# A delta-rule attention with two MoE layers: the first tile's x finished in PSUM, and the second MoE's second layer turned round

## The chip, the cores and the metric

The kernel runs on one core of a Trainium2 chip. The metric is the device time of one execution in microseconds (us). The kernel before was run three times: 1483.88, 1479.08 and 1480.54 us, median 1480.54. A core has TensorE (PE, matmuls; PEld is its weight load), VectorE (DVE), ScalarE (ACT), GpSimd (POOL) and SyncE (SP), which here only issues transfers (DMAs).

## The reference

Three layers follow one another, all in fp32: attention with a state that is corrected token by token, a gated MoE without experts, and an MoE of four experts that are all computed and weighted by given probabilities.

```
B, H, S, D = 4, 8, 768, 48                       # 3072 tokens, 384 = H * D
for t in range(S):                               # per batch and head, state 48 x 48
    y[:, :, t] = q[:, :, t] @ state              # reads before it writes
    v_old = kt @ state                           # kt: k of the token / (its norm + 1e-6)
    state = state + beta * outer(kt, vt - v_old)
x = y.transpose(0, 2, 1, 3).reshape(3072, 384)
h = x @ w_in                                     # 384 -> 2048
x = (h * sigmoid(1.702 * h)) @ w_out             # 2048 -> 384
p = probs / (probs.sum(-1) + 1e-9)               # 3072 x 4
out = 0
for e in range(4):
    out += p[:, e] * (relu(x @ w1[e]) @ w2[e])   # 384 -> 1024 -> 384
```

## The kernel before

**Numbers.** Every large operand is kept as two fp32r halves, hi (the rounded value) and lo (the rest), and each product of the MoE layers is three matmuls: hi x hi, hi x lo, lo x hi (`PASSES`). A "split" makes the pair: ScalarE (or VectorE) copies to hi, VectorE subtracts for lo.

**Attention.** The sequence is cut into 12 blocks u of 64 tokens. For each block the work is: normalise k; transpose it (`queue_keys`, L333); grams of k with k and of k with q (`queue_g` L511/L514, `queue_q` L444); invert a small triangular matrix for each batch and head (on GpSimd, or for blocks 0 and 1 on VectorE in two halves that PE merges, L661/L670, `queue_first_inverse`); and then the chain (`queue_chain`), which must run block after block because of the state: product of k and the state (L733), two solves (L743) with a cross product between (L753), `read` (L765: y from state and corrected values, both kept in `su`) and `write` (L770: the state's change). The 32 states of 48 x 48 (4 batches, 8 heads) lie as two times 16: heads in pairs x = 0, 1 on partitions 0 to 47 and 64 to 111. `read` gives y with d on the partitions, which is x^T, the form that the MoE's first layer takes as moving operand. Partitions 48 to 63 and 112 to 127 stay free; of four pairs of heads three fill the 48-row places (KD = 3 blocks of 128 rows), and the fourth pair's 48 rows are cut into three times 16 for the free places. For this, `y_copy` (L180 as helper) copies y to `stage` and the fourth pair to a scratch `YS`, and six DMAs a block (`put`, L848; for blocks 0 and 1 three on SP's queue and three on ACT's) move the pieces of 16.

**First MoE.** Six tiles t of 512 tokens (two blocks each, of four batches). `split_x` splits `stage` into `xs`; for each of 16 blocks f of 128 hidden units `layer1` (L884) makes `ph`, `gate` applies the gelu and splits it into `gh` (L987, L989, L990), and `layer2_1` (L972) sums `px` with the weights as the loaded operand. The second layer is one step behind the first, so that PE has work while the gate runs. Tiles 0 and 1 begin in halves of 256 columns (`HALVED`: 8 and 16 steps), so that the first half can start when one block of attention is done. The weights of this layer come as 64-bit floats that are converted on chip (L230, L277 and others).

**Order of work.** The attention of tile t + 2 is queued when tile t starts. A list scheduler written into the kernel (`Order`, `Task`) keeps a modelled clock for each engine and gives each piece a priority; `tick` in `layer1` and `layer2_1` lets pieces of attention in between MoE matmuls, and `until` runs the list up to given pieces. The resulting order on each engine is fixed when the kernel is built.

**Second MoE.** It runs expert by expert (e), tile by tile (t), in 8 steps f. The weights of all eight steps of an expert stay resident; those of the next are split during tile 5 (`queue_w2`). x of the tile is split two steps ahead (`split_now`, L1077/L1078) into one of two sets of buffers, `xsp` and `xs2`. `layer1` is the same function as in the first MoE, then a relu with split (L1112, L1113), and, a step later, `layer2_2` (L1086): for each batch b three matmuls of 384 columns with the hidden values as loaded operand, so that tokens lie on the partitions, into four of six PSUM buffers `po`. At the last step VectorE multiplies by the probability of each partition's token and adds to `oacc` (L1094), and for the last expert four DMAs write a tile. Between the two MoEs the PSUM pools change: `ps2`'s buffers can be used when the last `px` has been copied out, and VectorE does that copy after the three splits of the second MoE's first x.

Of the kernel before, what the change touches and what calls it, by code (L numbers as in the profile page):

```python
# [149 lines left out]
def delta_attention_moe_moe_kernel(  # L150
# [17 lines left out]
    E = probs.shape[1]  # L168
    F2 = we.shape[0] // E
# [52 lines left out]

    def load_w2(n):
        nc.sync.dma_start(out=raw[:, n % 2, :], in_=we[n])

    def split_w2(n):
        t = wp.tile([128, 2, 768], F32R, name="w", tag="w")
        half = raw[:, n % 2, :]
# [94 lines left out]
    V = nc.vector  # L323

# [98 lines left out]
    def queue_q(u):  # L423
# [11 lines left out]
        for g0 in range(0, NP, 8):  # L435
# [251 lines left out]
    def queue_chain(u):  # L687
# [27 lines left out]
        for hu in range(2):  # L715
# [65 lines left out]
            def s_add(x, gs=gs, cell=cell):  # L781
# [4 lines left out]
                else:  # L786
# [3 lines left out]
                               read=read, write=write, y_copy=y_copy, s_add=s_add))  # L790


        for hs in [halves[0:1], halves[1:2]] if u < 2 else [halves]:
# [29 lines left out]
            if n == 1:  # L823
                h, = hs
                reads = [task(h["read"], "PE", 1.0, (*bs, pdone[u]), prio=p, can=lambda: free_at("yg"))]
# [4 lines left out]
            for h, y in zip(hs, reads):  # L830
                ye = h["cell"]["yev"] = [task(lambda e, x=x, h=h: h["y_copy"](e, x), ("ACT", "DVE"), (0.7, 0.72), (y,), prio=p,
                                              can=y_free) for x in range(2)]
                wr = task(h["write"], "PE", 0.82, bs, prio=p) if n == 1 else reads[0]
# [7 lines left out]


        ov = []
        for x in range(2):
            for kk in range(KD):
                def put(x=x, kk=kk):
                    d, n = DR[x] + 16 * kk, DR[x] + D
                    (nc.scalar if u < 2 and x else nc.sync).dma_start(out=xst[n:n + 16, kk, u % 2], in_=YS[u][d:d + 16])  # L848

                ov.append(task(put, "ACT" if u < 2 and x else "HW", 0.45, yev, lat=2.3, prio=p, slack=5))  # L850
# [5 lines left out]
    xst = stage.rearrange("p (k c b i) -> p k c b i", k=KD, b=B, c=2)  # L856

# [31 lines left out]
    with tc.manual_schedule():  # L889
# [6 lines left out]
        nc.gpsimd.memset(SU, 0.0)  # L896
        m2 = scr[2][:, 0:C]
# [33 lines left out]
        x1 = {}  # L931
        x1d = [drx.tile([128, KD, TT], F32, name=f"x1d{t}") for t in range(KEEP)]
# [4 lines left out]
        def queue_w2(n):  # L937
            e, f = divmod(n, F2)
            WE[e, f] = split_w2(n)
            if n + 2 < E * F2:  # L940
                load_w2(n + 2)

        def x1_out(t):
# [16 lines left out]
            return ev  # L960

# [44 lines left out]
        def split_stage(t, cs, us, fs):  # L1006
            if not us:
                return split
            until(*(ydone[u] for u in us))
            if cs.start == 0:  # L1010
# [173 lines left out]
```

## Time and profile before

| | |
|---|---|
| median of three runs | 1480.54 us |
| profiled execution | 1484.33 us |
| its span, first to last instruction | 1482.6 us |
| mean granted TensorE clock | 0.974 of full speed |
| PE busy | 1420.4 us, 96% of the span |
| VectorE, ScalarE, GpSimd busy | 619.3, 459.8, 191.9 us |
| share of PE on the chain that ended last | 90% (L884 40%, L1086 27%, L972 13%) |

One execution is recorded by the hardware profiler. "Busy" counts time in which an engine has an instruction in work; PE's matmuls overlap, and a row's length runs to the end of its last matmul, so that the spacing of matmuls is read from starts, not from the mean length of one. The profile has a page of totals, and the trace behind it answers questions: a table of busy times by stretch, the order in time of one engine, groups of equal instructions, the DMAs, and the chain of waits followed back from the last instruction. An idle time is shown with what ended it.

### The profile page before, as it was taken

Reading aid. Unit: us, or ns where it says so; the run is one execution under the profiler, and the core shown is the slowest. Engines: PE = TensorE matmul, PEld = TensorE weight load, DVE = VectorE, ACT = ScalarE, POOL = GpSimd, SP = SyncE. Lnnn points to the kernel's source line nnn. Section 1 sums busy time; section 2 is a strip of 40 time slices with the busy share of each in tenths; the row PEclk is TensorE's granted clock in tenths of the full one; section 3 lists DMA queues with packets and bytes.
Section 4 is the critical chain, followed back from the end, with each engine's and each line's share of the span. In section 5 each row is a group of like instructions: output and inputs, shape, how many; then the busy total and the mean of one; then the engine's idle time right before and its main releaser. Section 6 shows DMA issues by size and latency. Waiting matters only on the chain.

```text
span 1482.6 us, 30388 instructions
## 1 busy us (share of the span) xinstructions
PE 1420.4 (96%) x13552; PEld 1258.2 (85%) x13552; DVE 619.3 (42%) x1033; ACT 459.8 (31%) x866; POOL 191.9 (13%) x340
## 2 busy tenths in 40 slices
PE   3687999999999999999999999999999999999999
PEld 2677889998888788888999999999999999999998
DVE  6978756545473423332223242232433223423222
ACT  5554434445353233432111231121321112222111
POOL 2019550080260530000000000000000000000000
PEclk8588999999999999999999999999999999999999
DMA  9211021201201000410000020000200000100001
GB/s 316 115 27 36 2 74 34 62 22 26 49 23 37 15 33 8 142 52 1 0 1 0 10 77 0 1 0 1 64 22 0 1 0 22 43 22 22 22 22 43
DMA packets 41331, 53.71 MB, mean 36 GB/s; under 512 B 25712, under 2 KB 29936, under 8 KB 41200
## 3 DMA queue, kind: packets, MB, share of 16 engines
q1 hardware_dynamic: 41008, 51.67, 11.7%
q8 instruction: 106, 1.74, 0.5%
q14 instruction: 25, 0.20, 0.0%
q10 hardware_dynamic: 192, 0.10, 0.0%
HBM read 42.71 MB, written 7.86 MB: 34 GB/s over the span
## 4 chain that ended last, share of the span: by engine, by line
PE 90%; DVE 2%; DMA 1%; ACT 1%; SPq 0%; issue 0%; DVEq 0%
PE ph L884 40%; PE po L1086 27%; PE px L972 13%; PE ch L743 2%; PE gp L444 2%; PE ch L733 1%; PE y L765 1%; DMA pq<-in_q_dram 1%; PE ch L753 1%; PE ch L770 1%; PE gp L511 1%; SPq L848 0%; DVE w L277 0%; DVE gh L990 0%; DVE scr L479 0%
## 5 line engine op out<-in xcount | busy, mean ns | idle before, releaser
L884 PE MATMUL ph<-xs,w 128*128 128x512 f32 (+1 forms) x2808 | 664.8, 379 | 3.7 <-DVE x L180 2.4
L884 PEld LDWEIGHTS ph<-xs,w 128*128 128x128 f32 x2808 | 499.7, 190 | 90.3 <-issue 2.8
L1086 PE MATMUL po<-w,hh 128*128 128x384 f32 x2304 | 432.8, 336 | 0.0
L1086 PEld LDWEIGHTS po<-w,hh 128*128 128x128 f32 x2304 | 407.6, 188 | 17.1
L1113 DVE SCALAR_TENSOR_TENSOR hh<-ph,hh 128x512 fp32r<-128x512 f32 x192 | 132.9, 692 | 554.0 <-ACT hh L1112 554.0
L1112 ACT ACTIVATE hh<-ph 128x512 fp32r<-128x512 f32 x192 | 115.0, 599 | 632.3 <-PE ph L884 632.3
L972 PE MATMUL px<-gh,w 128*128 128x512 f32 (+1 forms) x1080 | 233.5, 356 | 0.6 <-DVE gh L990 0.4
L972 PEld LDWEIGHTS px<-gh,w 128*128 128x128 f32 x1080 | 178.5, 192 | 29.4 <-DVE gh L990 2.0
L990 DVE TENSOR_TENSOR gh<-ph,gh 128x512 fp32r<-128x512 f32 (+1 forms) x120 | 69.5, 579 | 147.7 <-ACT gh L989 146.9
L987 ACT ACTIVATE ph<-ph 128x512 f32<-128x512 f32 (+1 forms) x120 | 59.5, 496 | 207.8 <-PE ph L884 203.5
L569 POOL TENSOR_TENSOR scr<-scr,itmp 128x30 f32<-128x30 f32 (+9 forms) x150 | 89.4, 596 | 11.8
L567 POOL TENSOR_TENSOR itmp<-scr 128x30 f32<-128x30 f32 (+9 forms) x150 | 81.4, 543 | 11.4
L989 ACT CAST gh<-ph 128x512 fp32r<-128x512 f32 (+1 forms) x120 | 60.2, 502 | 3.8
L180 ACT COPY su<-ch 32x384 f32<-32x384 f32 x77 | 36.2, 471 | 49.6 <-PE ch L743 45.0
L444 PE MATMUL gp<-pq,kt 48*64 48x64 f32 x768 | 34.2, 254 | 18.1 <-DMA pq<-in_q_dram 9.5
L444 PEld LDWEIGHTS gp<-pq,kt 48*64 48x64 f32 x768 | 31.3, 166 | 21.4 <-issue 8.3
L1078 DVE TENSOR_TENSOR xs<-x,xs 128x512 fp32r<-128x512 f32 x72 | 45.3, 684 | 2.0 <-ACT xs L1077 2.0
L511 PE MATMUL gp<-kt 48*32 48x64 f32 x768 | 28.2, 231 | 17.0 <-ACT kt L180 16.2
L743 PEld LDWEIGHTS ch<-v,scr 32*32 32x32 f32 x1536 | 36.5, 110 | 7.8 <-issue 4.6
L511 PEld LDWEIGHTS gp<-kt 48*32 48x32 f32 x768 | 25.2, 116 | 20.8 <-ACT kt L180 17.6
L743 PE MATMUL ch<-v,scr 32*32 32x48 f32 x1536 | 40.4, 208 | 0.7 <-DVE pq L449 0.5
L180 ACT COPY kt<-scr 32x512 f32<-32x512 f32 (+1 forms) x60 | 37.0, 617 | 12.0 <-DVE scr L333 11.1
(106 smaller groups left out, 809.6 us busy)
## 6 DMA issues: line engine op xcount, KB each, us to landing
raw<-in_we_dram SPq DMA_DIRECT2D x32, 384.0 KB, 3.1
rw<-in_w_dram SPq DMA_DIRECT2D x14, 768.0 KB, 12.2
k<-in_k_dram SPq DMA_DIRECT2D x12, 384.0 KB, 5.1
pq<-in_q_dram SPq DMA_DIRECT2D x24, 192.0 KB, 4.5
v<-in_v_dram SPq DMA_DIRECT2D x12, 384.0 KB, 3.2
out_dram<-oacc SPq DMA_DIRECT2D x24, 192.0 KB, 1.9
x1d<-raw SPq DMA_DIRECT2D x12, 256.0 KB, 2.3
x<-x1d SPq DMA_DIRECT2D x4, 768.0 KB, 5.8
```

Of the source, the lines that this page charges most:

```text
L180: (nc.scalar.copy if e == "ACT" else nc.vector.tensor_copy)(out=out_, in_=in_)
L444: mm(ps[TR[x]:TR[x] + C, i, :], lhsT=kt[d:d + D, g, :], rhs=pq[d:d + D, g, x, :], start=True, stop=True)
L511: mm(ps[r:r + SB, i, :], lhsT=kt[d:d + D, g, 0:SB], rhs=kt[d:d + D, g, :], start=True, stop=True)
L567: E.tensor_tensor(out=tv, in0=x[:, j:j + 1, j + 1:].broadcast_to([128, m, r]), in1=x[:, 0:m, j:j + 1].broadcast_to([128, m, r]), op=ALU.mult)
L569: E.tensor_tensor(out=x[:, 0:m, j + 1:], in0=x[:, 0:m, j + 1:], in1=tv, op=ALU.add)
L743: mm(cell["ps"][r:r + 32, i, :], lhsT=Tb[u][r:r + 32, g, :], rhs=V2[u][r:r + 32, g, :], start=True, stop=True, tile_position=(r, r))
L884: mm(ps, lhsT=w[:, a, kk * 128:(kk + 1) * 128], rhs=xs[kk][:, b, cs], start=kk == 0 and i == 0, stop=kk == KD - 1 and i == 2)
L972: mm(px[d][:, cs], lhsT=w[:, a, 384 + d * 128:384 + (d + 1) * 128], rhs=gh[:, b, 0:cs.stop - cs.start], start=f == 0 and i == 0 and cs.sta ...
L990: a = task(lambda: nc.vector.tensor_tensor(out=lo, in0=ph, in1=hi.bitcast(F32), op=ALU.subtract), "DVE", 0.07 + 0.53 * c, (a,), **kw)
L1086: mm(po[b], lhsT=hh[:, a, b * 128:(b + 1) * 128], rhs=w[:, c, 384:768], start=f == 0 and i == 0, stop=f == F2 - 1 and i == 2)
L1112: nc.scalar.activation(out=hh[:, 0, :], in_=ph, func=AF.Relu)
L1113: nc.vector.scalar_tensor_tensor(out=hh[:, 1, :], in0=ph, scalar=0.0, in1=hh[:, 0, :].bitcast(F32), op0=ALU.max, op1=ALU.subtract)
```

## The change

**First tile.** For blocks 0 and 1 the 16-row pieces of the fourth pair of heads are no longer moved by DMAs. A copy of its state columns, `fourth`, is put into `stage` in a place 64 columns wide whose first 48 are zero (`stage` is cleared by GpSimd at the start); `read` then multiplies this by the fourth pair's q into all 64 rows of y (L776), and adds the ordinary product over it (L777). y is complete x^T in PSUM. `take_x` makes hi from it and `take_rest` lo, straight into `xs0`. Other tiles go as before. `write` of blocks 0 and 1 now depends on `read`, and the k-q grams of blocks u > 1 may not be issued before the first MoE has begun.

**Second MoE.** Except for tile 5, `layer2_2` is turned: the weights are the loaded operand, the hidden values move, 3 x 3 matmuls of 512 columns; d lies on the partitions, and the probabilities are read as a row broadcast to all partitions (`load_pb`, from a normalised copy in DRAM). VectorE multiplies in PSUM (L1164) and adds to `oacc` (L1165); for the last expert it transposes a tile in blocks of 32 x 32 (L1170), and 16 DMAs write it. The columns of w2 are laid out for that on the host. Tile 5 keeps the old form as `layer2_last`. The next expert's weights are split in tiles 1 to 4.

**Between.** `xs2` is allocated before `big`, so that it lies beside the gate's buffers (`ghp`); the sets of x are used in the opposite order; and the first x of the second MoE is split at step 12 of the first MoE's last tile.

```diff
@@ queue_q (k-q gram)
-                         (*placed[u], lq, begun[0], *ends[-1:]), prio=p + 1, can=lambda: some_free(BANKS, whole))
+                         (*placed[u], lq, begun[0], *ends[-1:]), prio=p + 1,
+                         can=lambda: None if u > 1 and not od.moe else some_free(BANKS, whole))
@@ queue_chain, read
-                    mm(py[o:o + D, i, :], lhsT=SU[:, c0:c0 + D], rhs=pq[:, g, x, :], start=True, stop=True)
+                    if not t and g % 4 == KD:
+                        continue
+                    if not t:
+                        g3 = g - g % 4 + KD
+                        mm(py[o:o + C, i, :], lhsT=S4[:, g // 4, x, g % 4, :], rhs=pq[:, g3, x, :], start=True, stop=False)
+                    mm(py[o:o + D, i, :], lhsT=SU[:, c0:c0 + D], rhs=pq[:, g, x, :], start=bool(t), stop=True)
+            def take_x(e, kk, hu=hu, cell=cell):
+                c0 = (u % 2) * TT // 2 + hu * TT // 4
+                copy(e, xs0[kk][:, 0, c0:c0 + TT // 4].rearrange("p (b i) -> p b i", i=C),
+                     cell["py"].rearrange("p (b m) i -> p m b i", m=4)[:, kk])
...
-                wr = task(h["write"], "PE", 0.82, bs, prio=p) if n == 1 else reads[0]
+                wr = task(h["write"], "PE", 0.82, (y,), prio=p) if n == 1 else reads[0]
@@ between the MoEs
+                if t == NW - 1 and f == F1 - 4:
+                    first = [split_now(0, 0, kk) for kk in range(KD)]
...
-                xs2 = ctx.enter_context(tc.tile_pool(name="xs2", bufs=3))
@@ second MoE
+    pb[e, t] = raw[:, 1, 0:TT]
+    nc.sync.dma_start(out=pb[e, t], in_=prd[e:e + 1, t * TT:(t + 1) * TT].broadcast_to([128, TT]))
...
         def layer2_2(e, t, f, hh, w):
-            for b in range(B):
...
-                    mm(po[b], lhsT=hh[:, a, b * 128:(b + 1) * 128], rhs=w[:, c, 384:768],
+            for kk in range(KD):
...
+                    mm(po[kk], lhsT=w[:, a, 384 + kk * 128:384 + (kk + 1) * 128], rhs=hh[:, c, :],
                       start=f == 0 and i == 0, stop=f == F2 - 1 and i == 2)
...
+                    nc.vector.tensor_tensor(out=ps, in0=ps, in1=pb[e, t], op=ALU.mult)
+                    nc.vector.tensor_tensor(out=acc[:, kk], in0=acc[:, kk], in1=ps.rearrange("p (c j) -> p c j", j=32),
+                                            op=ALU.add)
+            if f == F2 - 1 and e == E - 1:
+                for h in range(2):
+                    half = oacc[t][:, h * KD * TT // 2:(h + 1) * KD * TT // 2]
+                    nc.vector.transpose(out=half, in_=half)
+        def layer2_last(e, t, f, hh, w):
+            acc = oacc[t].rearrange("p (b d) -> p b d", b=B)
...
+                       rhs=w[:, c, 384:768].rearrange("p (k a i) -> p a k i", a=4, k=KD),
```

Where the first MoE begins, TensorE had this before: the read of the block's first half (y), its write (`ch` from `su` and k), the merge of the second block's inverse (L661, L670), the second read, a gram of k with k (L511 and L514, 16 pairs of rows, of which one pair stands here), a gram with q, and the MoE's first two steps:

```order
L765 MATMUL y<-pq_78,su 48x64 x16
L770 MATMUL ch_652<-su,k_0_81 48x48 x16
L770 MATMUL ch_675<-su,k_0_81 48x48 x16
L661 MATMUL gp<-scr_100,scr_99 32x16 x64
L670 MATMUL gp<-scr_98,scr_100 32x16 x64
L765 MATMUL y<-pq_78,su 48x64 x16
L511 MATMUL gp<-kt_76 32x64 x2
L514 MATMUL gp<-kt_76 32x32 x2
...
L444 MATMUL gp<-pq_78,kt_76 64x64 x32
L884 MATMUL ph<-xs,w 128x256 x18
```

And now, with the reads' pairs of rows (24 products each, two pairs shown of the second), and the first of eight pairs of the gram:

```order
L799 MATMUL ch_656<-su,k_0_81 48x48 x16
L776 MATMUL y<-pq_78,stage 64x64
L777 MATMUL y<-pq_78,su 48x64
L776 MATMUL y<-pq_78,stage 64x64
L777 MATMUL y<-pq_78,su 48x64
...
L799 MATMUL ch_679<-su,k_0_81 48x48 x16
L518 MATMUL gp<-kt_76 32x64 x2
L521 MATMUL gp<-kt_76 32x32 x2
...
L931 MATMUL ph<-xs,w 128x256 x18
...
L668 MATMUL gp<-scr_100,scr_99 32x16 x64
L931 MATMUL ph<-xs,w 128x256 x7
L1029 MATMUL px_1017<-gh,w 128x256
L677 MATMUL gp<-scr_98,scr_100 32x16 x64
```

The merge (L668, L677 now), half of the k-k gram and the gram with q (L450 now, further on than the rows shown) have moved behind the first MoE matmuls, and each write stands behind its read.

Where tile 1 begins, TensorE had this before, from the reads of block 2's chain (`ch_2332`) over the start of block 3's (`ch_2663`) to the first matmul of tile 1's first half (256 columns wide), among steps of tile 0:

```order
L765 MATMUL y<-pq_78,su 48x64 x16
L884 MATMUL ph<-xs,w 128x512 x7
...
L733 MATMUL ch_2680<-su,kt_77 64x48 x16
L884 MATMUL ph<-xs,w 128x512 x2
L972 MATMUL px_1193<-gh,w 128x512 x3
L972 MATMUL px_1194<-gh,w 128x512 x3
L743 MATMUL ch_2663<-v_2523,scr_100 32x48 x16
L743 MATMUL ch_2680<-v_2523,scr_100 32x48 x16
L972 MATMUL px_1195<-gh,w 128x512 x3
L753 MATMUL ch_2663<-su,g 32x48 x16
L753 MATMUL ch_2680<-su,g 32x48 x16
L884 MATMUL ph<-xs,w 128x256 x9
```

And now (block 3's chain is `ch_2695` here):

```order
L1029 MATMUL px_1019<-gh,w 128x512 x3
L777 MATMUL y<-pq_78,su 48x64 x16
L799 MATMUL ch_2400<-su,k_2_83 48x48 x16
L799 MATMUL ch_2417<-su,k_2_83 48x48 x16
L777 MATMUL y<-pq_78,su 48x64 x16
L740 MATMUL ch_2695<-su,kt_77 64x48 x16
L740 MATMUL ch_2712<-su,kt_77 64x48 x16
L750 MATMUL ch_2695<-v_2591,scr_100 32x48 x16
L750 MATMUL ch_2712<-v_2591,scr_100 32x48 x16
L931 MATMUL ph<-xs,w 128x256 x9
```

Between the end of block 2's reads and tile 1's first matmuls there is no MoE work of tile 0 left, and of block 3's chain the product and one solve stand there, without the cross product.

In the last expert, VectorE had one instruction for each of four batches behind a tile's last step, between the low halves of the next tile's hidden values:

```order
L1094 SCALAR_TENSOR_TENSOR oacc<-po,pr,oacc 128x384 x4
L1113 SCALAR_TENSOR_TENSOR hh<-ph_12781,hh 128x512
L1113 SCALAR_TENSOR_TENSOR hh<-ph_12810,hh 128x512
L1113 SCALAR_TENSOR_TENSOR hh<-ph_12835,hh 128x512
L1113 SCALAR_TENSOR_TENSOR hh<-ph_12860,hh 128x512
```

And now (the number behind `oacc` is the tile's buffer):

```order
L1217 SCALAR_TENSOR_TENSOR hh<-ph_12598,hh 128x512
L1217 SCALAR_TENSOR_TENSOR hh<-ph_12620,hh 128x512
L1164 TENSOR_TENSOR po<-po,raw 128x512
L1165 TENSOR_TENSOR oacc_7903<-oacc_7903,po 128x16x32
...
L1170 STREAM_TRANSPOSE oacc_7903<-oacc_7903 128x768 x2
L1217 SCALAR_TENSOR_TENSOR hh<-ph_12666,hh 128x512
```

Six instructions (three pairs) and two transposes stand there now ahead of the next low half.

## Rows read from the trace of the kernel before

**Rows 1.** Page, busy time of each engine: us, share of the span, instructions.

```profile
PE 1420.4 (96%) x13552; PEld 1258.2 (85%) x13552; DVE 619.3 (42%) x1033; ACT 459.8 (31%) x866; POOL 191.9 (13%) x340
```

**Rows 2.** Table by stretch: us, busy of PE, PEld, DVE, ACT, POOL; PEclk, DMA, GB/s.

```profile
73.00:82.00 9.00, 3.48 (x143) 2.88 (x139) 7.41 (x16) 5.12 (x10) 0.00 (x0) 0.69 0.43 69
119.60:131.60 12.00, 4.16 (x68) 3.82 (x65) 11.86 (x16) 3.08 (x6) 10.98 (x14) 0.59 0.39 74
292.00:676.00 384.00, 379.17 (x4512) 315.20 (x4510) 169.82 (x273) 150.91 (x295) 102.05 (x186) 1.00 0.14 40
740.00:1400.00 660.00, 660.00 (x3317) 597.37 (x3316) 208.19 (x319) 141.22 (x239) 0.00 (x0) 1.00 0.06 17
```

**Rows 3.** PE in time, first tile: start, us, instruction, [idle before <-what ended it].

```profile
61.13 1.95 PE L765 MATMUL y<-pq,su 128*48 128x64 f32 x32
...
66.61 1.54 PE L661 MATMUL gp<-scr,scr 32*32 32x16 f32 x128 [1.61 <-DVE su L787]
...
82.94 3.67 PE L444 MATMUL gp<-pq,kt 48*64 48x64 f32 x62 [0.86 <-DMA pq<-in_q_dram]
86.55 4.21 PE L884 MATMUL ph<-xs,w 128*128 128x256 f32 x18
...
131.55 2.29 PE L884 MATMUL ph<-xs,w 128*128 128x256 f32 x9
```

**Rows 4.** PE in time, last tile of the first MoE: layer 1 of two following steps.

```profile
626.73 2.20 PE L884 MATMUL ph<-xs,w 128*128 128x512 f32 x9
...
630.81 2.20 PE L884 MATMUL ph<-xs,w 128*128 128x512 f32 x9
```

**Rows 5.** PE in time, second MoE: one step of both layers.

```profile
902.07 2.27 PE L1086 MATMUL po<-w,hh 128*128 128x384 f32 x12
904.18 2.24 PE L884 MATMUL ph<-xs,w 128*128 128x512 f32 x9
906.26 2.27 PE L1086 MATMUL po<-w,hh 128*128 128x384 f32 x12
```

**Rows 6.** Groups of equal instructions: busy us, mean ns | idle before <-what ended it.

```profile
L1113 DVE SCALAR_TENSOR_TENSOR hh<-ph,hh 128x512 fp32r<-128x512 f32 x192 | 132.9, 692 | 554.0 <-ACT hh L1112 554.0
L987 ACT ACTIVATE ph<-ph 128x512 f32<-128x512 f32 x72 | 41.9, 581 | 138.3 <-PE ph L884 134.2 <-DVE scr L590 2.9 <-DVE w L230 1.0
L333 DVE STREAM_TRANSPOSE scr<-k 128x512 f32<-128x512 f32 x24 | 16.0, 694 | 0.3
```

**Rows 7.** PE and SP's queue in time, chains of blocks 2 and 3.

```profile
174.51 2.07 PE L733 MATMUL ch<-su,kt 48*64 48x48 f32 x64
...
193.76 1.10 PE L765 MATMUL y<-pq,su 128*48 128x64 f32 x32
...
195.59 3.70 SPq L848 DMA_DIRECT2D stage<-scr  x6
...
203.69 1.55 PE L753 MATMUL ch<-su,g 32*32 32x48 f32 x64
205.17 1.10 PE L884 MATMUL ph<-xs,w 128*128 128x256 f32 x7
```

**Rows 8.** PE in time, start of the second MoE (two windows).

```profile
676.30 4.36 PE L884 MATMUL ph<-xs,w 128*128 128x512 f32 x18 [2.43 <-DVE x L180]
...
678.23 2.43 PE L884 MATMUL ph<-xs,w 128*128 128x512 f32 x10
680.50 0.69 PE L1086 MATMUL po<-w,hh 128*128 128x384 f32 x3
```

**Rows 9.** VectorE and SP's queue in time, first y copied and moved.

```profile
75.43 0.29 DVE L180 COPY scr<-y 48x128 f32<-48x128 f32 x1
...
74.95 1.84 SPq L848 DMA_DIRECT2D stage<-scr  x3
```

**Rows 10.** Chain of waits: start, us, a gram with q at full clock.

```profile
225.81 2.15 PE gp L444 x62
```

**Rows 11.** DMA issues: count, KB each, median us from issue to landing.

```profile
stage<-scr SPq DMA_DIRECT2D x66, 16.0 KB, 1.8
```

More of the change, by code (lines that the diff above doesn't have):

```diff
@@ L323, in delta_attention_moe_moe_kernel @@
     V = nc.vector
+    xs0 = [xsp.tile([128, 2, TT], F32R, name="xs", tag="xs") for _ in range(KD)]
+    direct = {}
     def queue_turn(u, k2t, deps, p):
@@ L789, in queue_chain @@
             halves.append(dict(hu=hu, cell=cell, ks=ks, rest=rest, solve=solve, solved=solved, cross=cross, rest2=rest2,
-                               read=read, write=write, y_copy=y_copy, s_add=s_add))
+                               read=read, write=write, y_copy=y_copy, s_add=s_add, fourth=fourth,
+                               take_x=take_x, take_rest=take_rest))
         for hs in [halves[0:1], halves[1:2]] if u < 2 else [halves]:
@@ L824, in queue_chain @@
                 h, = hs
-                reads = [task(h["read"], "PE", 1.0, (*bs, pdone[u]), prio=p, can=lambda: free_at("yg"))]
+                bs.append(task(h["fourth"], ("ACT", "DVE"), (0.35, 0.35), bs, prio=p))
+                reads = [task(h["read"], "PE", 1.5, (*bs, pdone[u]), prio=p, can=lambda: free_at("yg"))]
             else:
@@ L840, in queue_chain @@
         edone[u] = task(lambda: None, None, 0.0, ends, lat=0.0, prio=p)
+        if not t:
+            direct[u] = yev
+            ydone[u] = task(lambda: None, None, 0.0, yev, lat=0.0, prio=p)
+            return
         ov = []
@@ L847, in put @@
                     d, n = DR[x] + 16 * kk, DR[x] + D
-                    (nc.scalar if u < 2 and x else nc.sync).dma_start(out=xst[n:n + 16, kk, u % 2], in_=YS[u][d:d + 16])
-                ov.append(task(put, "ACT" if u < 2 and x else "HW", 0.45, yev, lat=2.3, prio=p, slack=5))
+                    nc.sync.dma_start(out=xst[n:n + 16, kk, u % 2], in_=YS[u][d:d + 16])
+                ov.append(task(put, "HW", 0.45, yev, lat=2.3, prio=p, slack=5))
         whole["end"] = ov
@@ L896, in delta_attention_moe_moe_kernel @@
         nc.gpsimd.memset(SU, 0.0)
+        nc.gpsimd.memset(stage, 0.0)
         m2 = scr[2][:, 0:C]
@@ L939, in queue_w2 @@
             WE[e, f] = split_w2(n)
-            if n + 2 < E * F2:
-                load_w2(n + 2)
+            m = n + 2 if n + 2 <= F2 else n + 1
+            if n != F2 - 1 and m < E * F2:
+                load_w2(m)
         def x1_out(t):
@@ L960, in x1_out, with split_now @@
             return ev
+        def split_now(n, t, kk):
+            s = (xsp if n % 2 else xs2).tile([128, 2, TT], F32R, name="xs", tag="xs")
+            src = x1[t][:, kk, :]
+            nc.scalar.copy(out=s[:, 0, :], in_=src)
+            nc.vector.tensor_tensor(out=s[:, 1, :], in0=src, in1=s[:, 0, :].bitcast(F32), op=ALU.subtract)
+            return s
         evac = []
@@ L1009, in split_stage @@
             until(*(ydone[u] for u in us))
+            if not t:
+                xs[:] = xs0
+                return [a for u in us for a in direct[u]]
             if cs.start == 0:
@@ L1072, in delta_attention_moe_moe_kernel, with load_pb @@
         po = {}
-        def split_now(n, t, kk):
-            s = (xs2 if n % 2 else xsp).tile([128, 2, TT], F32R, name="xs", tag="xs")
-            src = x1[t][:, kk, :]
-            nc.scalar.copy(out=s[:, 0, :], in_=src)
-            nc.vector.tensor_tensor(out=s[:, 1, :], in0=src, in1=s[:, 0, :].bitcast(F32), op=ALU.subtract)
-            return s
-        def layer2_2(e, t, f, hh, w):
+        pb = {}
+        def load_pb(n):
+            e, t = seq[n]
+            if t == NW - 1:
+                return
+            pb[e, t] = raw[:, 1, 0:TT]
+            nc.sync.dma_start(out=pb[e, t], in_=prd[e:e + 1, t * TT:(t + 1) * TT].broadcast_to([128, TT]))
@@ L1097, in layer2_2 @@
                         r0 = b * S + t * 128
-                        nc.sync.dma_start(out=out[r0:r0 + 128, :], in_=acc)
+                        nc.sync.dma_start(out=out[r0:r0 + 128, :], in_=acc[:, b])
         pend = None
         seq = [(e, t) for e in range(E) for t in range(NW)]
-        xs = [split_now(0, 0, kk) for kk in range(KD)]
+        load_pb(0)
+        pr5 = big.tile([128, E, B], F32, name="pr5")
+        for e in range(E):
+            nc.sync.dma_start(out=pr5[:, e], in_=prd[e, (NW - 1) * TT:].rearrange("(b p) -> p b", b=B))
+        xs = first
         for n, (e, t) in enumerate(seq):
```

94 lines of the change are left out of this document (71 added, 23 removed).

## Prediction

> **What bounds the kernel now.** I read the page's busy shares first: TensorE (PE) is busy for 1420.4 of the span's 1482.6 us [rows 1]. So only two things can pay: time in which PE waits, and time that its matmuls take beyond their columns. The table by stages says where the first lies: PE works 3.48 of 9 us from 73 to 82 us and 4.16 of 12 from 119.6 to 131.6, at a mean clock of 0.69 and 0.59, while from 292 to 676 us it misses under 5 of 384 us and from 740 to 1400 us nothing [rows 2]. The order in time of PE's work shows what ends those two waits: a gram of the *next* tile (L444) that waits for its q, the second time as the first, and behind it the first MoE's first tile, whose two halves start at 86.55 and 131.55 us [rows 3]. In the second MoE nothing waits, so there I look at the spacing of matmuls.
>
> **Turned second layer, spacing.** In the first MoE's last tile a step is 9 matmuls of 512 columns for layer 1 and 9 for layer 2 (weights as the loaded side), and takes 630.81 - 626.73 = 4.08 us, 227 ns a matmul [rows 4]. In the second MoE 12 matmuls of 384 columns take 904.18 - 902.07 = 2.11 us (176 ns each) and the 9 of layer 1 take 2.08 us, 231 ns each; a step is 4.19 us [rows 5]. Columns moved are 9 x 512 = 12 x 384 = 4608 in both. If a column costs 1/2.4 ns (the granted clock is 1.00 in both stretches), what is left is 227 - 213 = 13 to 14 ns a matmul in the first MoE, and in the second 16 and 18. Turning round takes away 3 matmuls a step (about 40 ns) and the change of width between the layers, which I hold to be what makes the second MoE's layer 1 slower than the same instructions in the first MoE. The new step is the first MoE's step, instruction for instruction: 4.08. Other steps of the second MoE are a little shorter than 4.19, so I take 0.10 us a step. Five of six tiles turn: 4 experts x 5 tiles x 8 steps = 160 steps, 16.0 us. The last tile of each expert stays as it is; its second operand is now read in pieces of 32 columns, which no row shows; I take nothing for it, with a bound of 10 ns a matmul at most (the jitter between 227 and 231 is 4), 384 x 10 ns = 4 us.
>
> The Trainium skill, "TensorE: Matmul & The Clock Gate", section "Wait — 56ns, not 53.3ns?", has it that matmuls start N / 2.4 GHz plus about 2.5 ns apart, whatever N. By that three matmuls fewer would be worth 7.5 ns a step, 1.2 us in all. The rows have 13 ns and more in the fixed part, so I go by the rows.
>
> **What the turned layer adds on VectorE.** The result now lies with d on the partitions, so the probabilities can't be a scalar per partition: each of three blocks takes a 128x512 multiply with a broadcast row, and for experts 1 to 3 an add, six instructions instead of four. I take 0.69 us for each (VectorE's 128x512 that reads PSUM [rows 6]). VectorE writes PSUM in no row; ScalarE does so in place in 0.58 us [rows 6], no slower than elsewhere, so I assume no surcharge. Is it hidden? Count from a tile's first matmul. The first low half ends at about 3.5 us, six instructions end at 7.7, the next low half at 8.4. PE needs that one after 5 half steps and a matmul, at 10.4. There are 2 us to spare. In the last expert two 128x768 transposes stand before that low half; by the 128x512 one (0.69 us) 1.04 each, so it ends at 10.4, just in time. I charge 0.1 us for each of five tiles: 0.5 us (bounds 0 and 3). The broadcast rows, weights and the smaller output pieces have most of a 33 us tile to land; 16 output DMAs at 0.6 us an issue (six puts took 3.70 us [rows 7]) take SP 10 us, and a row that waits behind them is read 20 us later.
>
> **Between the MoEs** PE waits 2.43 us, for a copy that stands on VectorE behind three splits of x [rows 8]. The splits now come four steps earlier, so the wait is one copy of 0.69 us and its hand-over, 0.9: gain 1.5 us (bounds 0.5 and 2.4). The first matmul also names DMA semaphores; they are of loads half a tile earlier.
>
> **The first tile.** Its x now comes straight from PSUM: no copies to staging, no six DMAs from 74.95 us on [rows 9], no split from staging. Block 0's first read starts at 61.13 as now [rows 3]; the new copy of the fourth head's state lies beside the other half's solve. Eight extra 64-wide products make 24 entries of 16: 1.95 x 1.5 = 2.9 us, to 64.1. Three casts and three subtractions of under 0.3 us (a 128-wide copy of y takes 0.29 [rows 9]) stand on VectorE behind key work and free y's bank at 66.8; second read to 69.8, write 1.0, one gram about 1.5: first MoE matmul at 72.3 instead of 86.55. The gram of block 2 (3.67) and the merge of block 1's inverse (first part 1.54, after a wait of 1.61) are gone from ahead of it [rows 3].
>
> From there to the end of the second read, where the second wait opens (119.6 [rows 2]), PE took 119.6 - 86.55 = 33.1 us [rows 3]. Added to it now are the moved things: block 2's gram at 2.15 (its length at full clock [rows 10]), two merge products 3.1, one gram 1.0, half more reading 1.1. 72.3 + 40.4 = 112.7. VectorE's list up to there sums to 38 us, and its last subtractions stand behind two masks and a weight split, which costs PE about 2.3: second half at 115.0 instead of 131.55. Block 3's gram (2.15) now follows it instead of preceding it: 14.4 us ahead.
>
> Not all of that lasts. Tile 1's first half needs block 2's chain, which still goes over DMAs. The order puts its first product two steps (8.2 us) later among the MoE steps than now: 115.0 + (174.51 - 131.55) + 2.15 + 8.2 = 168.3. To the end of the second read it takes 194.86 - 174.51 = 20.4 now [rows 7], less 15 MoE matmuls that no longer lie between (3.4): 185.3. Then 0.7 to the first of six puts, 3.7 for their issue, 1.8 for landing [rows 11], 0.8 for the split: 192.3. Now that half starts at 205.17, with one product of 1.55 more behind it, so 203.6 to compare: **11 us** are left. PE has too little else to do there and waits some 5 us. Bounds: 4 (all of VectorE's load ends late by as much as one wait of 6.8 us now) and 15 (nothing lost at tile 1). Later tiles have slack: their chains stand between MoE steps as before. One memset more on GpSimd (about 1.4 us) delays masks that are read 8 us later.
>
> **Sum.** 11 + 1.5 + 16.0 - 0.5 = 28.0 us. Against the profiled execution (1484.33 us, span 1482.6) this is 1456.3; the median of the three runs is 3.8 lower, 1480.54, so **1452.5 us**. Bounds added: 4 + 0.5 + 9 (16 less 4 less 3) = 13.5 and 15 + 2.4 + 16.5 = 34, so 1467 to 1446.5.
>
> **Rivals.** (a) *The spacing does not improve.* If the 231 ns of the second MoE's layer 1 belong to that stage and not to the change of width, a step is 18 x 231 ns = 4.16 and 160 steps give 4 us: 1480.5 - 11 - 1.5 - 4 = 1464. For it: the same instructions are slower there today. Against: the stage opens with 18 of them after a wait, and the last ten start from 678.23 on until the first matmul of layer 2 at 680.50, 227 ns apart [rows 8]: without a change of width they come down to the first MoE's spacing. By the skill's 2.5 ns it would be 1467.
>
> (b) *The start's gain is eaten.* Tile 1 can't start before block 2's chain; if that waits for VectorE, busy 11.86 of 12 us before the second half now [rows 2], 2 of 11 us stay: 1461.5. Against: VectorE has no staging copies left, and fewer weights to split by then.
>
> (c) *Slower: VectorE late with the low half.* A multiply into PSUM could cost more than 0.69. From 1.05 us each on, the 2 us are used up; at 1.4 each of 10 tiles of experts 1 and 2 loses 2.2 us and each of 5 of expert 3 4.3: 43 us against 28, 1495. It turns slower from about 1.2 us each. Against: every 128x512 on VectorE or ScalarE here lies at 0.58 to 0.69 [rows 6].
>
> (d) *All of the start stays* (15 of 15): 1448.5, inside the range.
>
> **Numbers.** Forecast 0.66, (a) 0.10, (b) 0.12, (c) 0.05, (d) 0.07. The range 1445 to 1466 takes in (a), (b) and (d) and leaves (c) and mixtures. About 0.3% (4.4 us) is what can be told from no change. Forecast, (a), (b), (d) are all faster: 0.95, with 0.02 off for mixtures; same 0.03, slower 0.04.
>
> **What would show it.** Steps of the second MoE at 4.08 us, matmuls of po and ph alike at 227 ns, and 4.18 in every sixth tile; first MoE matmul near 72, second half near 115, tile 1 near 192 with some 5 us of PE idle ahead that ends on a DMA or split; under 1 us before the second MoE. Wrong if PE waits on VectorE in the first two steps of a tile, or if ph keeps 231 ns.

## The result

The changed kernel took 1457.85, 1453.96, 1461.59 and 1466.76 us, median 1459.72; the kernel before, in four runs, 1481.52. The ratio is 0.9857 (95% interval 0.9826 to 0.9887). The profiled execution is the one of 1457.85 us (span 1456.1): 1.6 us above the forecast for a profiled execution, while the median is 7.2 above the forecast median, inside its range. That the profiled time came so close is luck: the sum hides two errors against each other. The spread of the changed kernel, 13 us where that of the kernel before is 5, is a third finding.

Page of the changed kernel, busy time (the row that answers to [rows 1]):

```profile
PE 1404.5 (96%) x13136; PEld 1194.3 (82%) x13136; DVE 648.1 (45%) x1067; ACT 457.7 (31%) x867; POOL 191.3 (13%) x341
```

All MoE steps are the same in both kernels and come in the same order, so their starts can be compared one by one. "Lead" is how much earlier the changed kernel starts the same step. The pieces of attention between the steps do not stand in quite the same places: at tile 0's second half and at tile 1's first and ninth steps the changed kernel has 64 small matmuls (a gram or a cross product, 1.5 to 2.1 us) still to do that the kernel before has behind it, so that the lead in work is some 16.5, 12.6 and 5.4 us there. From tile 1's second half, ninth step, on the work is the same.

| step | before | after | lead |
|---|---|---|---|
| first MoE, tile 0, first half | 86.55 | 68.94 | 17.6 |
| tile 0, second half | 131.55 | 112.93 | 18.6 |
| tile 1, first step | 205.17 | 190.99 | 14.2 |
| tile 1, ninth step | 242.48 | 235.53 | 7.0 |
| tile 1, second half, ninth step | 302.47 | 297.19 | 5.3 |
| tile 3, ninth step | 463.62 | 458.14 | 5.5 |
| tile 4, first step | 517.63 | 508.86 | 8.8 |
| tile 5, ninth step | 638.97 | 629.75 | 9.2 |
| second MoE, first step | 676.30 | 665.48 | 10.8 |
| last matmul's end | 1479.03 | 1452.75 | 26.3 |

TensorE at the start, at tile 1 and behind it, changed kernel, in order of time (columns as in [rows 3]):

```profile
68.94 0.38 PE L931 MATMUL ph<-xs,w 128*128 128x256 f32 x1
69.89 2.28 PE L931 MATMUL ph<-xs,w 128*128 128x256 f32 x17 [0.56 <-DVE xs L793]
...
168.18 2.07 PE L740 MATMUL ch<-su,kt 48*64 48x48 f32 x64
...
183.91 1.10 PE L777 MATMUL y<-pq,su 128*48 128x64 f32 x32
...
187.78 1.14 PE L740 MATMUL ch<-su,kt 48*64 48x48 f32 x32 [1.59 <-DVE su L813]
188.85 2.21 PE L750 MATMUL ch<-v,scr 32*32 32x48 f32 x64
190.99 0.58 PE L931 MATMUL ph<-xs,w 128*128 128x256 f32 x1
193.50 2.08 PE L931 MATMUL ph<-xs,w 128*128 128x256 f32 x8 [1.93 <-DVE xs L925]
195.50 2.77 PE L760 MATMUL ch<-su,g 32*32 32x48 f32 x64
...
224.18 2.08 PE L450 MATMUL gp<-pq,kt 48*64 48x64 f32 x62 [2.01 <-DMA pq<-in_q_dram]
```

Block 2's chain starts at 168.18 and its second read ends at 185.0, as forecast (168.3 and 185.3). Two waits stand there, 1.59 us ahead of tile 1 and 1.93 inside its first step. Look at the lengths behind them: the 64 matmuls of the cross product (L760, L753 before) take 2.77 us at 195.50 and 1.55 before [rows 7]. The table by stretch says why. 187 to 207 us, first the kernel before, then the changed one; the third figure from the right is the granted clock:

```profile
187.00:207.00 20.00, 20.00 (x385) 16.38 (x385) 9.95 (x21) 6.24 (x16) 17.49 (x33) 1.00 0.29 68
```

```profile
187.00:207.00 20.00, 17.29 (x257) 14.91 (x259) 6.78 (x13) 6.76 (x14) 10.45 (x21) 0.57 0.32 78
```

From about 190 us, behind the first wait and ahead of the second, until about 206 us TensorE ran at the lower of its two levels, 1.2 GHz (0.50). The lead of 14.2 us shrinks to 7.0 within eight steps (in work, from 12.6 to 5.4).

Between tiles 3 and 4 the lead grows by 3.3 us without an edit: in the profile of before a gram waits there 1.45 us for its q, with a stretch at half clock behind it (497 to 500 us at 0.55), and in the profile after it does not. The chain of waits of the kernel before:

```profile
491.22 5.02 DMA pq<-in_q_dram
496.29 2.84 PE gp L444 x62
```

The same transfer takes 4.1 us from issue to landing in the profile after, and 4.2 in that of start_undone below, whose attention stands in the order of before and where the gram waits 0.25 us. The kernel before has one profile, so how often it waits that long is not known from it.

The second MoE of the changed kernel, TensorE and VectorE at the first steps of a tile of the last expert (answers to [rows 5]):

```profile
1286.43 2.20 PE L931 MATMUL ph<-xs,w 128*128 128x512 f32 x9
1288.47 2.20 PE L1156 MATMUL po<-hh,w 128*128 128x512 f32 x9
1290.52 2.20 PE L931 MATMUL ph<-xs,w 128*128 128x512 f32 x9
...
1296.63 2.20 PE L1156 MATMUL po<-hh,w 128*128 128x512 f32 x9
```

```profile
1289.91 0.69 DVE L1164 TENSOR_TENSOR po<-po,raw 128x512 f32<-128x512 f32 x1
...
1294.02 1.84 DVE L1170 STREAM_TRANSPOSE oacc<-oacc 128x768 f32<-128x768 f32 x2
1295.78 0.65 DVE L1217 SCALAR_TENSOR_TENSOR hh<-ph,hh 128x512 fp32r<-128x512 f32 x1
```

A step is 4.09 us (1286.43 to 1290.52; 4.08 on the mean of a tile), and nothing waits: the low half ends at 1296.43, and the first matmul that reads it is the second at 1296.63, at 1296.86. Between the MoEs the wait of 2.43 [rows 8] is now

```profile
665.48 4.36 PE L931 MATMUL ph<-xs,w 128*128 128x512 f32 x18 [0.83 <-ACT x L181]
```

### The profile page after: what moved, and what is told of

The parts are those of the page before. It is cut to its first block, busy times and chain, and to the rows that moved or that the text cites. A ratio compares the mean times of both kernels' runs of the same rounds, so it can differ in the third digit from the quotient of the medians.

```text
span 1456.1 us, 29677 instructions
## 1 busy us (share of the span) xinstructions
PE 1404.5 (96%) x13136; PEld 1194.3 (82%) x13136; DVE 648.1 (45%) x1067; ACT 457.7 (31%) x867; POOL 191.3 (13%) x341
## 4 chain that ended last, share of the span: by engine, by line
PE 90%; DVE 3%; issue 1%; DMA 1%; ACT 0%; SPq 0%; DVEq 0%
PE ph L931 40%; PE po L1156 22%; PE px L1029 13%; PE po L1186 5%; PE ch L750 2%; PE y L777 2%; PE ch L740 1%; PE ch L760 1%; PE ch L799 1%; PE gp L518 1%; PE gp L450 1%; DVE w L281 1%; DMA pq<-in_q_dram 0%; DVE gh L1047 0%; DVE rw L273 0%
## 5 line engine op out<-in xcount | busy, mean ns | idle before, releaser
L931 PE MATMUL ph<-xs,w 128*128 128x512 f32 (+1 forms) x2808 | 655.6, 376 | 4.8 <-DVE xs L925 3.0
L1156 PE MATMUL po<-hh,w 128*128 128x512 f32 x1440 | 352.4, 389 | 0.0
L1156 PEld LDWEIGHTS po<-hh,w 128*128 128x128 f32 x1440 | 270.3, 188 | 56.1
L1186 PE MATMUL po<-w,hh 128*128 128x384 f32 x384 | 73.9, 342 | 0.0
L1186 PEld LDWEIGHTS po<-w,hh 128*128 128x128 f32 x384 | 69.3, 188 | 2.4
L181 ACT COPY kt<-scr 32x512 f32<-32x512 f32 (+1 forms) x58 | 35.8, 617 | 15.7 <-DVE scr L339 14.8
```

The source lines that it names most:

```text
L181: (nc.scalar.copy if e == "ACT" else nc.vector.tensor_copy)(out=out_, in_=in_)
L931: mm(ps, lhsT=w[:, a, kk * 128:(kk + 1) * 128], rhs=xs[kk][:, b, cs], start=kk == 0 and i == 0, stop=kk == KD - 1 and i == 2)
L1156: mm(po[kk], lhsT=w[:, a, 384 + kk * 128:384 + (kk + 1) * 128], rhs=hh[:, c, :], start=f == 0 and i == 0, stop=f == F2 - 1 and i == 2)
L1186: mm(ps, lhsT=hh[:, a, b * 128:(b + 1) * 128], rhs=w[:, c, 384:768].rearrange("p (k a i) -> p a k i", a=4, k=KD), start=f == 0 and i == 0, ...
```

## The experiments

Theory: the first tile's gain was there, and was lost at tile 1 to two waits that the order makes, and more to the half clock behind them. Rivals: block 2's chain can't be earlier because VectorE, GpSimd or the transfers bound it; or the gain only moves from wait to wait.

**The change once more** (change_again, no edit).

> The changed kernel once more, to see which of its times repeat. If the loss of tile 1 is a fixed feature of the order (a wait of PE of some 3.5 us for block 2's x, then about 15 us at half clock, 0.50), the profile shows the first MoE matmul near 69, tile 1 near 191 and its ninth step near 235 again, and the times lie from 1454 to 1467. If it was an accident of that one execution, tile 1's ninth step comes near 228 and the time near 1450.

Six times: 1456.91 to 1459.82 four times, 1468.47 and 1469.76; median 1459.23. The profiled one is that of 1469.76, and tile 1 comes later in it than expected (202.34, ninth step 246.81). Its lead at tile 0's second half is 7.6 us instead of 18.6, and from there on it loses at tile 1 what the first profile lost (11.9 us there from tile 0's second half to tile 1's ninth step, 11.7 in the first). In late_split, turn_undone and extra_evacuation below, whose attention stands in the same order, that loss is 7.7, 11.7 and 17.0 us. So tile 1's loss belongs to the order, though not its exact size, and there is a second one, which of the ten profiles with the first tile's change only this one has. The two executions, merge of block 1's inverse, first the changed kernel's profile, then this one:

```profile
83.40 0.87 PE L677 MATMUL gp<-scr,scr 32*32 32x16 f32 x82 [0.77 <-issue]
```

```profile
84.84 0.86 PE L677 MATMUL gp<-scr,scr 32*32 32x16 f32 x82 [1.00 <-issue]
```

Table by stretch, from there on, second execution:

```profile
84.00:107.00 23.00, 22.16 (x354) 20.08 (x354) 10.16 (x18) 8.31 (x18) 0.00 (x0) 0.55 0.01 2
```

In the midst of 128 small matmuls TensorE stood still, 1.00 us in place of 0.77, waiting for nothing that the profile shows, and then ran at 0.55 on the mean for 23 us (1.00 in the first profile). From tile 0's first half to its second the lead falls by 8.8 us here and grows by 1.0 in the first profile, so this is some 10 of the 11.9 us between the two profiled times; whether the other times near 1469 have the same stretch no profile shows. What decides was not settled, and the length of the pause alone does not: in turn_undone the same pause took 1.44 us, and the clock stayed at 1.00 behind it.

```profile
83.94 0.87 PE L677 MATMUL gp<-scr,scr 32*32 32x16 f32 x82 [1.44 <-issue]
```

**Filler** (filler). 16 and 20 matmuls that compute nothing used, in the two waits:

```diff
+                reads.append(task(lambda: [hs[1]["read"](), idle(16 if u == 2 else 0)], "PE", 1.0, reads,
...
+                if t == 1 and cs.start == 0 and f == 0:
+                    idle(20)
```

> The changed kernel with matmuls on a spare buffer in the two waits ahead of tile 1: 16 of 256 columns (1.9 us) behind block 2's second read and 20 (2.4 us) ahead of tile 1's first step. They do no work that is used. Theory (what costs most is the half clock behind the waits, about 7.5 us, not the waits themselves, 3.5): the granted clock stays at 1.00 from 186 to 206 us, tile 1's ninth step comes near 228 to 229 instead of 235.5, and the time falls by 6 to 7 us. Rival (the waits alone are the loss, the clock costs nothing): no change, or 1 us slower.

```profile
187.00:207.00 20.00, 20.00 (x431) 18.55 (x430) 10.29 (x20) 8.94 (x21) 10.84 (x21) 1.00 0.41 108
```

The clock stayed at 1.00. From tile 1's first step to its fourth it took 14.8 us (194.68 to 209.51) instead of 23.2 (190.99 to 214.16), so the step that began 3.7 us later came 4.7 earlier. The same four steps take 19.6 to 23.0 us in the four other profiles of this order (change_again, late_split, turn_undone, extra_evacuation), and 14.9 in inverse_cost_1_2 below, where the clock stays at 1.00 too. From the end of block 2's second read to the fourth step it is 23.0 us instead of 29.1, although the filler itself takes 4.6 us and the two waits 3.5. At the ninth step 3.4 are left (232.18; forecast 228 to 229), since the gram with q behind it now waits with the clock falling there. Median 1456.33, five runs, some 3 us below the change: half of what was expected, and not clear of noise (ratio to before 0.9844, interval 0.9823 to 0.9866, beside 0.9873, interval 0.9844 to 0.9902). The profiles show that the idle time of 3.5 us was the smaller part of the loss at tile 1.

**The order at tile 1** (inverse_cost_1, inverse_cost_1_2, inverse_cost_1_35). GpSimd ends block 2's inverse long before VectorE's transpose that takes it, which stands late in VectorE's list because the planner counts that inverse at 1.5 times its cost:

```profile
151.24 1.92 POOL L580 TENSOR_TENSOR scr<-scr,bt 128x1024 f32<-128x1024 f32 x1
...
165.60 2.22 DVE L597 STREAM_TRANSPOSE scr<-scr 128x1024 f32<-128x1024 f32 x1
```

```diff
-            last = task(lambda j=j: step(j), "POOL", (0.52 + 0.0037 * m) * (1.5 if w == 2 else 1.0), (last,), prio=p)
+            last = task(lambda j=j: step(j), "POOL", (0.52 + 0.0037 * m) * (1.2 if w == 2 else 1.0), (last,), prio=p)
```

(1.0 and 1.35 in the others.)

> The changed kernel with the planner's cost of block 2's inverse on GpSimd at its plain value instead of 1.5 times it, so that block 2's chain is placed about two MoE steps earlier; GpSimd was done 12 us before the instruction that takes its result. Theory (start's gain is lost at tile 1 to a wait of 3.5 us and the half clock behind it): both go, tile 1 starts near 187 with no idle time ahead of it and clock 1.00, the lead over the kernel before at tile 1's second half is 14 to 17 us instead of 4.6, and the time falls by 9 to 12 us, to about 1448. Rival (VectorE and the transfers bound block 2's chain, not the order): the chain starts little earlier, the wait stays, under 2 us. Second rival: the lead is given back at the next wait, for q of the tile after it, 2 us now: 5 us are left.

> The changed kernel with the planner's cost of block 2's inverse at 1.2 instead of 1.5 times its plain value. At 1.0 the chain's first product stood so early that PE waited 4.3 us for a copy of block 2's grams; at 1.5 it stands 8 us too late and PE waits 3.5 us for x, with about 15 us at half clock behind it. Theory (both waits come from where the order puts the chain): at 1.2 neither is there, tile 1 starts near 186 to 188 at clock 1.00, and the time is 6 to 9 us below the changed kernel in executions that do not lose time elsewhere, near 1450. Rival (what is gained at tile 1 is only moved to the waits of tiles 1 and 2, for q and for x, as in the run at 1.0): within 3 us of the changed kernel.

> The same with 1.35 times: the chain one MoE step earlier than in the changed kernel. Theory: the wait ahead of tile 1 shrinks from 3.5 us to under 1, no half clock behind it, 5 to 8 us below the changed kernel. Rival (moved, not saved): within 3 us.

At 1.0: median 1464.13 (1457.23 to 1472.21), no gain. The wait ahead of tile 1 is gone, but the chain now stands too early and waits for the grams' copy, and what was gained is lost there and at later waits (for the next tile's x 1.44 us, for a q 1.37): at tile 4, where both have done the same work, the lead is 8.4 us, in the changed kernel 8.8. This one goes to the rival.

```profile
157.62 3.65 PE L740 MATMUL ch<-su,kt 48*64 48x48 f32 x64 [4.30 <-ACT g L181]
```

At 1.35: 1459.00 (1457.42 to 1470.89), no gain: there is still no MoE work between the second read and block 3's product, which waits, and the clock falls as in the changed kernel:

```profile
189.60 1.71 PE L740 MATMUL ch<-su,kt 48*64 48x48 f32 x32 [1.74 <-DVE su L813]
```

```profile
187.00:207.00 20.00, 18.26 (x277) 16.10 (x274) 7.83 (x15) 7.27 (x16) 10.70 (x21) 0.57 0.26 67
```

At 1.2: 1450.19 (1448.5 to 1452.48), ratio to before 0.9782 (0.9767 to 0.9797). The product stands at 157.35 and waits for nothing, tile 1 starts at 188.25 without idle time, and the clock stays:

```profile
157.35 2.07 PE L740 MATMUL ch<-su,kt 48*64 48x48 f32 x64
...
188.25 1.34 PE L931 MATMUL ph<-xs,w 128*128 128x256 f32 x9
```

```profile
187.00:207.00 20.00, 20.00 (x450) 18.18 (x445) 8.98 (x17) 10.16 (x25) 17.62 (x31) 1.00 0.43 107
```

Its lead at the second MoE's first step is 18.9 us, where the changed kernel has 10.8. Of the four orders this is the fastest, and its interval lies clear of the changed kernel's (0.9826 to 0.9887).

**Is 1.2 just better?** (before_cost_1_2: the same edit in the kernel before; start_undone_1_2 and inverse_cost_1_2_again: without the first tile's change, and with it, on one chip.)

> The kernel before with the planner's cost of block 2's inverse at 1.2 instead of 1.5, nothing else. Theory (1.2 pays in the changed kernel because it removes the wait ahead of tile 1, which the kernel before does not have): the time stays within 4 us of the kernel before. Rival (1.2 is simply a better order for both, so that the 9 us of the run at 1.2 say nothing about what the first tile's change lost): 6 to 10 us faster than the kernel before.

> The changed kernel without the first tile's change, and with the planner's cost at 1.2: the fourth corner of a square (first tile changed or not, cost 1.5 or 1.2, second MoE changed in all). So far: not changed at 1.5 1462.4, changed at 1.5 1459.2, changed at 1.2 1450.2; the kernel before gained 6.5 us by 1.2. If the two edits just add, 1456 here, and the first tile is worth 3 us at 1.5 and 6 at 1.2. Theory (the forecast's 11 us were there, and the order at 1.5 ate them at tile 1): 1459 to 1462, worth 9 to 12 at 1.2. Rival (the first tile is worth 3 us in either order): 1453.

> The changed kernel at 1.2 once more, on the same chip as the run without the first tile's change, for the difference of the two. If the small spread of its five times (1448.5 to 1452.5) is a feature, again within 1446 to 1454 and none near 1460 or above.

The kernel before gained too: 1477.32 beside 1483.87, ratio 0.9958 (0.9943 to 0.9972), 6.5 us, where the theory had less than 4. That is the rival's figure: its grams with q no longer wait (0.46 and 0.99 us at 224 to 226 before, and 1.45 at 496, none now). So not all that 1.2 gives is what the change had lost. Without the first tile's change it gives 1459.57 (1458.07 to 1461.60), with it 1455.17 (1448.64 to 1464.97): the small spread was not a feature, three of the six came at 1451.23 or below and three at 1459 to 1465. The medians differ by 4.4 us, which is not clear of noise (ratios to before 0.9850, interval 0.9833 to 0.9867, and 0.9825, interval 0.9793 to 0.9857); the three lower times lie 8 to 11 below 1459.57. In the profiles the leads at the second MoE's first step are

| | cost 1.5 | cost 1.2 |
|---|---|---|
| first tile as before | 7.4 | 9.4 |
| first tile changed | 10.8 | 18.9 and 17.5 |

so there the first tile's change is worth 3.4 us in the order that was handed over and 8.1 to 9.5 at 1.2; by the profiles the two edits need each other.

**Without the first tile's change** (start_undone: the old read, copies, DMAs and the free gram with q back).

```diff
-                        mm(py[o:o + C, i, :], lhsT=S4[:, g // 4, x, g % 4, :], rhs=pq[:, g3, x, :], start=True, stop=False)
-                    mm(py[o:o + D, i, :], lhsT=SU[:, c0:c0 + D], rhs=pq[:, g, x, :], start=bool(t), stop=True)
+                    mm(py[o:o + D, i, :], lhsT=SU[:, c0:c0 + D], rhs=pq[:, g, x, :], start=True, stop=True)
```

> The changed kernel without the change of the first tile (x of tile 0 goes over staging and the six DMAs again, the grams with q are not held back), the second MoE and the piece between as changed. Forecast's terms: the first tile is worth 11 us, so 1470; by the profile after, where the lead falls to 5.3 us behind tile 1, 1463 to 1466. If the first tile's part is worth nothing on the mean of executions (its times lie between 1454 and 1470), 1458 to 1461, with a smaller spread than the changed kernel.

1462.42 (1461.05 to 1465.73), ratio 0.9864 (0.9848 to 0.9880), beside 0.9857 and 0.9873 of the changed kernel: on the median of executions the first tile's change was worth from nothing to 3 us. Its own profile has the old start again (first MoE matmul at 85.53) and none of the loss at tile 1. It also has a lead over the profile of before, without the first tile's change: 3.2 us behind tile 1 and 7.4 at the second MoE. So of the 5.3 and 10.8 us in the table above, 2.1 and 3.4 are left for that change.

**Without the turned layer** (turn_undone).

```diff
-                    (layer2_last if pend[1] == NW - 1 else layer2_2)(*pend)
+                    layer2_last(*pend)
```

> The changed kernel with the second MoE's second layer in the old form in all tiles (hidden values loaded, 384 columns), the rest of the change as it is. Theory (the turned layer is worth 0.10 us a step, 15.6 us in the profile): steps of 4.17 to 4.20 us in the second MoE in all tiles, and 15 to 17 us slower than the changed kernel, about 1475. Rival (the steps are shorter because of the split of weights in other tiles, or of the place of the buffers): steps stay at 4.08 and the time within 4 us.

1479.93 (1477.34 to 1493.24), ratio to before 1.0010 (0.9986 to 1.0034): 20 us slower than the change (expected 15 to 17). In the profiles, from the second MoE's first matmul to the last it takes 805.4 us, in the changed kernel 787.3, in the kernel before 802.7. So turning is worth 15.5 us against the old form, and 2.7 more against the form that reads w in pieces of 32 columns. One step of it:

```profile
901.69 2.31 PE L1186 MATMUL po<-w,hh 128*128 128x384 f32 x12
903.84 2.20 PE L931 MATMUL ph<-xs,w 128*128 128x512 f32 x9
905.88 2.32 PE L1186 MATMUL po<-w,hh 128*128 128x384 f32 x12
```

Layer 1 takes 2.04 us (227 ns a matmul) directly behind matmuls of another width, layer 2 2.15 (179 ns).

**The splits between the MoEs** (late_split: `first` back behind the last matmuls).

> The changed kernel with the second MoE's first three splits of x put back behind the first MoE's last matmuls. If the 1.6 us between the two MoEs come from those splits on VectorE: PE waits 2.4 us there instead of 0.83, and nothing else changes. If they come from the buffers' place, the wait stays under 1 us.

```profile
664.14 5.97 PE L931 MATMUL ph<-xs,w 128*128 128x512 f32 x18 [2.39 <-issue]
```

The wait is 2.39 us again, so it was the splits. Here the 18 matmuls took 5.97 us instead of 4.36: from 1.5 us behind the wait on eight of them came 427 ns apart, 512 columns at 1.2 GHz, so half the clock. The early splits were worth 3.2 us in this pair of profiles, where the kernel before, with a wait of 2.43 and no fall of the clock, lost 1.6. Median 1461.73 of four (1458.15 to 1479.69), too wide for 1.6 or 3.2 us.

**VectorE's room in the second MoE** (extra_evacuation).

```diff
                     nc.vector.tensor_tensor(out=ps, in0=ps, in1=pb[e, t], op=ALU.mult)
+                    nc.vector.tensor_copy(out=ps, in_=ps)
```

> The changed kernel with one more copy in place (PSUM to PSUM, 128 x 512, VectorE) behind each multiply of experts 1 to 3, three for each turned tile. It measures the room that VectorE has behind a tile's last step. By the profile after, the next low half ends 2.2 us before TensorE wants it in experts 1 and 2 and 0.4 us before in expert 3, and three copies at 0.6 to 0.69 take 1.8 to 2.1: no wait in experts 1 and 2, about 1.5 us in each of five tiles of expert 3, 7 to 8 us in all (up to 15 if the clock falls behind each wait). Rival (what stands on VectorE there is hidden by more than the order shows): no change.

```profile
1305.69 2.12 PE L1156 MATMUL po<-hh,w 128*128 128x512 f32 x8 [1.67 <-DVE hh L1218]
```

Four waits of 1.67 and one of 1.43 us, all in expert 3, 8.1 us in sum, none in experts 1 and 2. Three copies of 0.70 are 2.1; less the 0.43 us of room that the profile after shows, that is 1.67. The clock does not fall behind these waits:

```profile
1260.00:1450.00 190.00, 181.90 (x808) 150.59 (x807) 79.68 (x119) 34.06 (x59) 0.00 (x0) 1.00 0.12 26
```

Median 1471.67 (1466.67 to 1479.46), 12 us above the change and more than expected. The second MoE of the profile is 10.7 us longer than the changed kernel's: 9.6 at the five waits, each 1.4 to 1.7 us of idle time and up to 0.3 more, and 1.1 in small steps before them. What the rest of the median's difference is stays open.

## Why the prediction was right, and where it was not

**Turned layer: right, 15.5 for 16.0.** Steps of 4.08 us at 160 places, as the first MoE's. The reason was right in its larger part only: fewer and wider matmuls (9 of 512 at 227 ns instead of 12 of 384 at 174.5 on the mean) are 0.054 us a step, and layer 1, which went from 231.7 ns on the mean to 226.7, is 0.045. That the change of width by itself makes layer 1 slower is refuted: in turn_undone and in tile 5 it runs at 227 with the change of width still there. What set the 231 in the kernel before is open. In tile 5 layer 2's matmuls start 179 ns apart instead of 174.5, inside the bound of 10, and with layer 1's at 227 a step is 4.19 us, 4.18 before. The Trainium skill, "TensorE: Matmul & The Clock Gate", section "Wait — 56ns, not 53.3ns?", would have given 1.2 us, an estimate from its 2.5 ns a matmul. The profiles with and without the turned layer differ by 15 and 18, and 227 ns is 13 above 512 columns at 2.4 GHz, so for these matmuls the measurement stands against the 2.5 ns.

**VectorE's lateness: 0 for 0.5.** The multiply in PSUM took 692 ns (forecast 690), two transposes 1.84 (2.08); the room was 0.43 us in the last expert, and extra_evacuation shows that it is no more than that.

**Between the MoEs: right**, 1.6 for 1.5, by the wait (2.43 to 0.83), and by late_split.

**The first tile: this step failed.** Forecast were the first MoE matmul at 72.3 (measured 68.94, and 69.89 for the rest of its step), second half at 115.0 (112.93), tile 1 at 192.3 (190.99 and 193.50), some 5 us of idle time ahead of it (3.5): every time up to tile 1 is within 4 us. The failed sentence is the next: "**11 us** are left". On its own count (from 203.6) 12.6 us were left at that point, or 10.1 by the rest of the step at 193.50, and 5.3 within 110 us. The idle time was counted as what it lasts, and not with what follows it: some 16 us at half clock, of which the filler gave back some 6 (29.1 us to 23.0). The Trainium skill, "TensorE: Matmul & The Clock Gate", section "Terms", prices throttled time at that time times the missing share of the clock; with the row of 187 to 207 us that is an estimate of 20 x (1 - 0.57) = 8.6 us. The filler's 6 lie somewhat below it, and 1.93 us of that stretch TensorE was idle. The rows to see the loss were there: the two waits of the start were read with a mean clock of 0.69 and 0.59 [rows 2], and those of a later wait (2 us at 0.50 behind the gram of 225.81 [rows 10]) were there to be asked for.

So rival (b) came true in its outcome (it said that 2 of the 11 us stay; against start_undone 2.1 to 3.4 stayed in the profiles, below the bound of 4, and 0 to 3 on the median) and not in its mechanism: VectorE's load did not bound the chain, since with the chain placed earlier TensorE waited for nothing at tile 1, and 8.1 to 9.5 us stayed.

**Profile and median.** Profile against profile the sum was 28.0 and the lead 26.3: of the start's missing 5.7 a part was covered by 3.3 us that the profile of before lost at a wait for q and the profile after did not. Without them the lead would be 23.0. Whether they are an accident of that one profile is not shown, and the medians speak rather against it: start_undone lies some 20 us below the kernel before, and the turned layer and the early splits account for 17.1 of them. The median of the changed kernel may also hold executions with a stretch of half clock at 86 to 107 us, which cost some 10 us in the one that was profiled. A term is checked on its own stretch, not on the sum.

## What to carry to other kernels

An idle time on TensorE costs more than its length when the clock falls behind it: price a new wait with the granted clock of the stretch that follows a wait of that kind in the trace, and see whether other work of the order can stand in it. Not every wait of that length has such a fall behind it: the five of extra_evacuation, 1.43 to 1.67 us among 512-wide matmuls, left the clock at 1.00. When an early stage gets faster, look at the order's modelled costs behind it: a figure that leaves 12 us of slack on one engine (1.5 for GpSimd's inverse) can set when the chain starts, and the best of four values is neither the plain one (1.0: too early, other waits) nor near the old (1.35: the same hole). And compare the starts of the same steps in two profiles, at places where both have done the same work, since two sums can agree by accident.

## What was not expected of the hardware

A pause in the midst of a run of small matmuls, which ends on nothing the profile shows, is followed in one of ten profiles, where it took 1.00 us, by 23 us at a mean clock of 0.55, and in the nine others, where it took 0.73 to 1.44 us, by no fall up to 105 us; the waits of 2.43 and 2.39 us between the MoEs likewise, none in the kernel before and half clock in late_split. Matmuls of 384 columns with a contiguous moving operand started 170 to 185 ns apart (174.5 on the mean) and 175 to 180 (179.4) with the operand in pieces of 32 columns, while the 512-wide ones behind them went from 231.7 to 226.7: the two forms cost nearly the same a step (4.18 and 4.19).
